# Seven block products for Q in the first half too, with every instruction of the schedule put at a new place

## The chip, the cores and the metric

The kernel runs on one core of a Trainium2 chip. The time is device microseconds from the first to the last instruction of an execution, with the little that lies around them; it is the median of several executions. The profile is of one execution.

## The reference

The input x has 2048 rows of 640. Everything works on its layer norm xn.

- Attention: Q = xn·wq, for 32 heads of 128. Only the last 512 keys and values of the cache are used. Per head, softmax(Q·Kᵀ/√128)·V, then the heads' results times wo, summed over the heads.
- Gate: relu(xn·w1 + b1)², times w2, plus b2, through silu, with 1728 hidden columns.
- Output: x + attention · gate.

All of it is in float32. TensorE multiplies a rounded kind of float32 (fp32r), so each operand is split into a high part and a low remainder, and each product is made of three matmuls: high·high, high·low, low·high (`triple`, L601).

## The kernel before

**Tiles and stages.** The rows of x are four tiles of 512. First comes the gate: tile 0 with plain products, tiles 1 and 2 together with seven block products in place of eight (a Winograd form of Strassen's scheme, on 2×2 blocks), then their second products in 28 steps of `c_down`, during which the layer norm of tile 3 is made. Then comes attention in 128 **units** (L997 and after); a unit is one head times one tile. The first 64 units (first half) take tiles 0 and 3, the last 64 (second half) tiles 1 and 2. Four units in a row, two heads times two tiles, make a group; there are 16 groups to a half.

**A unit.** TensorE makes 12 matmuls of scores (`s_mm`, four chunks of keys, three matmuls each), 12 of softmax times V (`v_mm`), Q for a later unit (`q_mm`, 15 matmuls; in the second half `q_prod` and `q_rest`), and a share of the output product (`r_mm`, 30 matmuls for each pair of heads and tile). VectorE folds the maximum over the keys out of each chunk's scores (`max_fold`), subtracts it (`shift`), adds up; ScalarE takes the exponentials and splits off high parts; GpSimd makes the low parts.

**Q in the second half.** Two heads are one block dimension, two tiles the other, and the contraction over 640 is two blocks of 256 and a rest of 128. With the weights' sums s1 to s4 and the tiles' sums t1 to t4, a group's Q takes 7 products of 6 matmuls and 4 rests of 3: 54 matmuls in place of 60. The weights' sums are made by GpSimd in the first half, when the same heads' weights are there anyway (`q_sums`), and stored to DRAM; in the second half they are loaded in four pieces (`q_piece`).

**What sets the order.** All work of attention is entered in a list with a time in a nominal unit of PERIOD = 12.4 (`at`, `on`), and a table K of some hundred small numbers moves single entries. The list is sorted by that time (L2007) and the calls are made in that order; every engine then takes its instructions strictly in it. The nominal times have no other effect.

**The slots of TensorE's code.** TensorE's instruction stream is fetched in blocks of 256 slots. Each matmul of the program becomes two instructions, a weight load and a matmul, one slot each; a wait for more than one semaphore adds slots of its own, one for each two further semaphores. `addr_align(256, slot)` asks that the next instruction stand at that slot of a block; the stream is filled up to it with empty instructions, up to 255 of them. In attention each unit asks for five places:

```
SLOTS = (0, 11, 22, 33, 42)
for c in range(KC):
    on(0.68 * c, align, i, SLOTS[c])
    on(0.68 * c, s_mm, i, c)
on(0.68 * KC - 0.6, align, i, SLOTS[KC])
# align: pe.addr_align(256, (188 + 128 * i + slot) % 256)
```

So a unit has 128 slots. The four chunks of scores begin 11 slots apart, and each is 6 slots of instructions and 5 of fill, when nothing else stands between. After the fifth place 86 slots are left for the other 42 matmuls of a unit of 54 (84 slots). If the stream is already past the place that is asked for, it is filled up to that place in the next block. The steps of `c_down` ask for places of their own (`lead_slot`), and the last of them, slot 139 before step 20, is followed by 150 matmuls up to unit 0.

Of the kernel before, what the change touches and what calls it, by code (L numbers as in the profile page):

```python
# [8 lines left out]
F32 = mybir.dt.float32  # L9
# [5 lines left out]
P = 128  # L15
NT = 512
# [2038 lines left out]
```

## Time and profile before

| | |
|---|---|
| median of 3 runs | 1973.06 us (1970.76 to 1973.12) |
| profiled execution, its own time | 1971.29 us |
| its span | 1969.5 us, 30081 instructions |
| TensorE (PE) busy | 1939.7 us, 98%, 8489 matmuls |
| VectorE (DVE) busy | 1708.3 us, 87% |
| GpSimd (POOL) busy | 1479.0 us, 75% |
| ScalarE (ACT) busy | 1394.5 us, 71% |
| mean granted TensorE clock | 0.995 |

All instructions are recorded under one line, that of a helper that fixes the order (L127), so the rows are told apart by the names of their tiles: s are scores, q Q, pq the bank in which Q is made, pt the split exponentials, o softmax times V, ot the split result of two heads, r their output product, acc the sum, e the shifted scores and exponentials, rdm and rds the folds. PE rows are matmuls, PEld rows weight loads. A matmul's duration in a row is longer than the distance to the next one, since they overlap. The gate takes the first 290 us, attention the time up to about 1880 us.

### The profile page before, as it was taken

How to read it: one execution, taken by the hardware profiler on the slowest of the kernel's cores; microseconds unless marked ns; L12 is line 12 of the kernel's file. 1: busy time of each engine (PE TensorE's matmuls, PEld its weight loads, DVE VectorE, ACT ScalarE, POOL GpSimd, SP SyncE). 2: the span in 40 equal slices, each digit the busy share in tenths (PEclk: the TensorE clock that was granted, in tenths of full speed). 3: DMA queues.
4: the chain of work that ended last, by engine and by line, in shares of the span. 5: the costliest groups of instructions: out<-in, count | busy, mean ns of one | idle time of the engine just before them, and what ended most of it. 6: DMA issues, size and time to landing. Idle time of an engine off the chain costs nothing. (4 is left out here: it accounts for less than half of the span.)

```text
span 1969.5 us, 30081 instructions
## 1 busy us (share of the span) xinstructions
PE 1939.7 (98%) x8489; PEld 1588.9 (81%) x8489; DVE 1708.3 (87%) x2915; ACT 1394.5 (71%) x2994; POOL 1479.0 (75%) x895
## 2 busy tenths in 40 slices
PE   9999999799999999999999999999999999999998
PEld 7888887588888888888888888888888888888787
DVE  6864747599999999999999989999999999999865
ACT  5675538577777777777777787777777777777743
POOL 1022118599999999999998688999998888888952
PEclk9999999899999999999999999999999999999999
DMA  6865953132222222333323333333332222222355
GB/s 204 278 227 206 369 184 120 64 97 97 97 97 97 97 97 97 99 107 108 106 97 110 116 126 99 105 105 105 105 114 84 84 84 84 83 84 89 123 180 192
DMA packets 149025, 246.89 MB, mean 125 GB/s; under 512 B 13876, under 2 KB 70726, under 8 KB 147846
## 3 DMA queue, kind: packets, MB, share of 16 engines
q1 hardware_dynamic: 144998, 229.87, 35.5%
q0 software_dynamic: 3728, 14.94, 2.0%
q8 instruction: 78, 1.28, 0.3%
q14 instruction: 77, 0.63, 0.1%
q10 hardware_dynamic: 144, 0.16, 0.0%
HBM read 175.97 MB, written 68.96 MB: 124 GB/s over the span
## 5 line engine op out<-in xcount | busy, mean ns | idle before, releaser
L127 POOL TENSOR_TENSOR pt<-e,pt 128x1024 fp32r<-128x1024 f32 x256 | 616.8, 2410 | 146.7 <-ACT pt L127 143.8
L127 PE MATMUL r<-ot,wo 128*128 128x512 f32 x1920 | 496.5, 392 | 3.0 <-DVE q L127 3.0
L127 PEld LDWEIGHTS r<-ot,wo 128*128 128x128 f32 x1920 | 361.5, 188 | 83.3 <-DVE q L127 3.5
L127 PE MATMUL o<-pt,wv 128*128 128x512 f32 x1536 | 395.3, 395 | 2.2 <-POOL pt L127 2.2
L127 PE MATMUL s<-q,wk 128*128 128x512 f32 x1536 | 371.9, 391 | 15.5 <-issue 15.5
L127 DVE TRANSPOSE_TENSOR_REDUCE rdm<-s 128x16 f32<-128x512 f32 x512 | 349.0, 713 | 35.1 <-PE s L127 33.5
L127 PEld LDWEIGHTS s<-q,wk 128*128 128x128 f32 x1536 | 289.5, 189 | 77.7 <-issue 16.2
L127 PEld LDWEIGHTS o<-pt,wv 128*128 128x128 f32 x1536 | 287.0, 188 | 72.2 <-POOL pt L127 7.0
L127 DVE TENSOR_TENSOR e<-s,bm 128x512 f32<-128x512 f32 x512 | 317.5, 655 | 2.5 <-POOL pt L127 0.7
L127 POOL TENSOR_TENSOR e<-e,e 128x1024 f32<-128x1024 f32 x128 | 307.9, 2405 | 8.9
L127 ACT ACTIVATE e<-e 128x1024 f32<-128x1024 f32 x256 | 269.7, 1054 | 32.8 <-DVE e L127 32.0
L127 ACT ACTIVATE pt<-e 128x1024 fp32r<-128x1024 f32 x256 | 271.5, 1060 | 16.1 <-PE o L127 0.9
L127 DVE TENSOR_TENSOR acc<-r,acc 128x512 f32<-128x512 f32 x300 | 203.4, 678 | 35.8 <-PE r L127 30.6
L127 PE MATMUL pq<-ax,wq 128*128 128x512 f32 x960 | 231.4, 389 | 0.0
L127 PEld LDWEIGHTS pq<-ax,wq 128*128 128x128 f32 x960 | 180.1, 188 | 37.9 <-DVE q L127 0.3
L127 ACT ACTIVATE rdm<-rdm 32x64 f32<-32x64 f32 x384 | 97.8, 255 | 97.3 <-DVE rdm L127 92.6
L127 ACT ACTIVATE rowm<-rowm 32x16 f32<-32x16 f32 x384 | 82.1, 214 | 89.6 <-DVE rowm L127 86.5
L127 DVE TRANSPOSE_TENSOR_REDUCE rds<-e 128x32 f32<-128x1024 f32 (+1 forms) x128 | 123.8, 968 | 17.2 <-POOL e L127 16.8
L127 ACT ACTIVATE rds<-rds 32x32 f32<-32x32 f32 (+1 forms) x384 | 89.4, 233 | 54.4 <-DVE rds L127 49.9
L127 ACT ACTIVATE rows<-rows 32x16 f32<-32x16 f32 x384 | 82.2, 214 | 60.5 <-DVE rows L127 52.0
L127 DVE TENSOR_TENSOR o<-o,bs 128x512 f32<-128x512 f32 x128 | 88.7, 693 | 11.0 <-PE o L127 3.9
L127 POOL TENSOR_TENSOR wo<-or,wo 128x640 fp32r<-128x640 f32 x62 | 97.4, 1571 | 0.0
(463 smaller groups left out, 2877.7 us busy)
## 6 DMA issues: line engine op xcount, KB each, us to landing
or<-in_wo_dram SPq DMA_DIRECT2D x62, 320.0 KB
qp<-wq_d SPq DMA_DIRECT2D x30, 640.0 KB
kr<-in_kT_dram SPq DMA_DIRECT2D x62, 256.0 KB
vr<-in_v_dram SPq DMA_DIRECT2D x62, 256.0 KB
wq_d<-ss SPq DMA_DIRECT2D x60, 256.0 KB
qp<-wq_d SPq DMA_DIRECT2D x30, 512.0 KB
wq_d<-wq SPq DMA_DIRECT2D x30, 384.0 KB
qr<-in_wq_dram SPq DMA_DIRECT2D x32, 320.0 KB
```

The costliest lines, as they stand in the source:

```text
L127: ins = method(*args, **kwargs)
```

## The change

- **Q in the first half.** From group 2 on (unit 8), the first half's Q also comes from seven products; only groups 0 and 1 keep `q_mm` (`NQS = UPG * G`). That takes 14 times 6 = 84 matmuls out: 8405 in place of 8489.
- **Tile sums for tiles 0 and 3.** `outer_sum`, `outer_hi`, `outer_lo` make t1 to t4 for these tiles during steps 10 to 18 of `c_down`: 12 sums and 8 low parts of 128×512 on VectorE, 8 high parts on ScalarE; 8 loads of tile 0 and 16 stores of 256 KB on GpSimd's queue. Six tiles of sums stay in SBUF in each half (`open_t`).
- **Weight sums.** `stage_raw` to `part_keep` take the place of `q_sums` to `q_store`. For all 16 groups the weights are loaded, summed, split and stored, and both halves load the pieces: 1051 DMA issues on SP's queue in place of 752.
- **Score banks in pairs.** A tile of scores now spans two banks. `max_fold` and `shift` work on 128×1024: 2 instructions each per unit in place of 4.
- **SBUF.** pt, the tile sums and other moving operands come to stand at multiples of 512 bytes; in the built program the 1536 matmuls that read pt had it 128 bytes beyond one, and 288 that read tile sums 256 bytes beyond one. The split results stay in four fixed tiles.
- **Places.** K has 1380 entries in place of 280, most of them for single units (`@56`), and a third set, part 2, for units 6 to 63.

The diff, cut to its core:

```diff
-    -0.06, "Q41": 1.2, "Q51": 0.05, "Q61": -0.15, "Q71": 0.17, "Q81": -0.21, "Q91": -0.62,
...
+    "Q8@59": 0.5, "Q8@63": -1.37, "Q8@67": 2.27, "Q8@7": -1.15, "Q91": 0.28, "Q92": 0.33,
+    "Q920": -1.66, "Q9@124": -0.99, "Q9@56": 0.14, "Q9@60": 0.05, "Q9@64": 0.08, "R00": -0.38,
...
+    def outer_sum(q, k):
+        if k == 0:
+            outer_tiles(q)
+        t0, t1, t2, t3 = (raw(t[1]) for t in TO[q])
+        x, b12, b22 = XO[q], XC[LATE, q], XC[LATE, NQ2 + q]
+        out, one, two, op = (
+            (t0, b12, x[:, 0, 0, :], ALU.subtract),
...
+        ENG["o"].tensor_tensor(out, one, two, op=op)
...
+    def outer_lo(q, j):
+        hi, lo = TO[q][j]
+        ENG["l"].tensor_tensor(lo, raw(lo), raw(hi), op=ALU.subtract)
+        for i in range(2):
+            pool.dma_start(TS_d[0][j][:, q, i, :], raw(TO[q][j][i]))
...
-    NQS = NU // 2 - UPG
+    NQS = UPG * G
...
+    def stage_lo(g, k):
+        hi, s = ST[g, k]
+        pool.tensor_tensor(s.bitcast(F32R), s, raw(hi), op=ALU.subtract)
...
+    def stage_keep(g, k):
+        n, lo = SUM_AT[k]
+        for i, src in enumerate((raw(ST[g, k][0]), ST[g, k][1])):
+            sp.dma_start(wq_d[g][n][:, i, lo : lo + NQ2, :], src)
...
     def s_mm(i, c):
         hf, g, t, h = units[i]
-        SC[i, c] = pools["psb"].tile([P, NT], F32, tag="s", name=f"s{i}_{c}", bufs=KC)
+        if c % 2 == 0:
+            SC[i, c // 2] = pools["psb"].tile(
+                [P, 2, NT], F32, tag="s", name=f"s{i}_{c}", bufs=KC // 2
+            )
...
-    def shift(i, c):
...
+    def shift(i, k):
...
+        dve.tensor_tensor(
+            E[i, k], SC.pop((i, k)), MB[i][:, None, :].to_broadcast([P, 2, NT]), op=ALU.subtract
+        )
...
+        part = 0 if i < NQS - 2 else 2 if i < NU // 2 else 1
+
         def key(name, when, u=0):
             return sum(
-                (K.get(f"{name}{k}", 0.0) for k in (hf, f"{hf}{(i + u) % UPG}", f"@{i + u}")), when
+                (K.get(f"{name}{k}", 0.0) for k in (part, f"{part}{(i + u) % UPG}", f"@{i + u}")), when
             )
...
-        if NG <= n < HALF * NG:
+        if NQS // UPG <= n < HALF * NG:
...
                 on(key("Q9", 2.75), q_prod, n, 2, "a", 3, "t3")
...
-        for c in range(KC):
-            on(0.8 + 0.68 * c, max_fold, i, c)
+        for k in range(KC // 2):
+            on(key(f"mf{k}", 1.5 + 1.3 * k), max_fold, i, k)
```

The order of TensorE's instructions, at three places. An ISA row is an `addr_align`; it takes no slot itself, and what it fills isn't shown. A MATMUL row is two slots for each matmul.

The first place is unit 8, the first whose scores stand beside the new Q products. Before, its second to fourth chunks of scores, each with its place ahead of it:

```order
L127 ISA
L127 MATMUL s8_1_4124<-q8_0_3931,wk0_4_0_3873 128x512
L127 MATMUL s8_1_4124<-q8_1_3932,wk0_4_0_3873 128x512
L127 MATMUL s8_1_4124<-q8_0_3931,wk0_4_1_3874 128x512
L127 ISA
L127 MATMUL s8_2_4136<-q8_0_3931,wk0_4_0_3873 128x512
L127 MATMUL s8_2_4136<-q8_1_3932,wk0_4_0_3873 128x512
L127 MATMUL s8_2_4136<-q8_0_3931,wk0_4_1_3874 128x512
L127 ISA
```

Now the same chunks (`s8_2` is the pair of banks of chunks 2 and 3; `ta` holds the tile sums, `pq2a` is Q's bank):

```order
L312 ISA
L312 MATMUL s8_0_4156<-q8_0_4096,wk0_4_0_3940 128x512
L312 MATMUL s8_0_4156<-q8_1_4097,wk0_4_0_3940 128x512
L312 MATMUL s8_0_4156<-q8_0_4096,wk0_4_1_3941 128x512
L312 ISA
L312 MATMUL s8_2_4171<-q8_0_4096,wk0_4_0_3940 128x512
L312 MATMUL s8_2_4171<-q8_1_4097,wk0_4_0_3940 128x512
L312 MATMUL s8_2_4171<-q8_0_4096,wk0_4_1_3941 128x512
L312 MATMUL pq2a_3909<-ta_3068,qp2_2_4026 128x512 x6
L312 ISA
L312 MATMUL s8_2_4171<-q8_0_4096,wk0_4_0_3940 128x512
```

The six matmuls of the product with t3 (Q9 at 2.75 + 0.33 − 1.66 = 1.42) have come ahead of the fourth chunk's place (2.04). They make 12 slots, and two waits 2 more, where 5 slots were free: 20 slots stand where 11 are asked for, so the stream is filled up with 256 − 9 = 247 empty instructions. The same stands in every fourth unit from 8 to 60, 14 times.

The second place is unit 4, before, where three matmuls of scores and six of the output product stand between two places:

```order
L127 ISA
L127 MATMUL s4_0_3543<-q4_0_3365,wk0_2_0_3307 128x512
L127 MATMUL s4_0_3543<-q4_1_3366,wk0_2_0_3307 128x512
L127 MATMUL s4_0_3543<-q4_0_3365,wk0_2_1_3308 128x512
L127 MATMUL r1_0_3547<-ot0_3301,wo0_0_0_3110 128x512 x2
L127 MATMUL r1_0_3547<-ot0_3301,wo0_0_1_3111 128x512
L127 MATMUL r1_0_3547<-ot1_3440,wo0_1_0_3256 128x512 x2
L127 MATMUL r1_0_3547<-ot1_3440,wo0_1_1_3257 128x512
L127 ISA
L127 MATMUL s4_1_3559<-q4_0_3365,wk0_2_0_3307 128x512
```

These are 18 slots where 11 are asked for, and 249 are filled; it is the only such place before. Now the rows read:

```order
L312 ISA
L312 MATMUL s4_0_3594<-q4_0_3414,wk0_2_0_3371 128x512
L312 MATMUL s4_0_3594<-q4_1_3415,wk0_2_0_3371 128x512
L312 MATMUL s4_0_3594<-q4_0_3414,wk0_2_1_3372 128x512
L312 ISA
L312 MATMUL s4_0_3594<-q4_0_3414,wk0_2_0_3371 128x512
L312 MATMUL s4_0_3594<-q4_1_3415,wk0_2_0_3371 128x512
L312 MATMUL s4_0_3594<-q4_0_3414,wk0_2_1_3372 128x512
L312 ISA
```

Here nothing stands between, and the fill is 5 again.

The third place is the way into attention, with the semaphores that an instruction waits for. Before, the first Q product and the first scores; 150 matmuls and 5 waits stand between slot 139 and slot 188, and no fill is needed (139 + 305 = 444 = 256 + 188):

```order
L127 MATMUL py2_4_2537<-ch26_1_2828,cw26_0_2831 128x512
L127 MATMUL py2_4_2537<-ch26_0_2827,cw26_1_2832 128x512
L127 MATMUL pq0_2899<-ax0_0_0_2735,wq0_2797 128x512 [waits DMASW4_49,DMASW5_49,DMASW3_49,DMASW6_49,DMASW2_49,DMASW7_49,DMASW1_49,DMAHW1_49,DMASW0_49,PE_49]
L127 MATMUL pq0_2899<-ax0_0_1_2736,wq0_2797 128x512 [waits DMAHW1_49]
L127 MATMUL pq0_2899<-ax0_0_0_2735,wq0_2797 128x512 x2
```

Now:

```order
L312 MATMUL py2_4_2593<-ch26_1_2891,cw26_0_2894 128x512
L312 MATMUL py2_4_2593<-ch26_0_2890,cw26_1_2895 128x512
L312 MATMUL pq0_2977<-ax0_0_0_2840,wq0_2898 128x512 [waits DMASW5_49,DMASW4_49,DMASW6_49,DMASW3_49,DMASW7_49,DMASW2_49,DMAHW0_49,DMASW1_49,DMAHW3_49,DMASW0_49,DMAHW5_49,PE_49,Activation_49]
L312 MATMUL pq0_2977<-ax0_0_1_2841,wq0_2898 128x512 [waits DMAHW6_49]
L312 MATMUL pq0_2977<-ax0_0_0_2840,wq0_2898 128x512 [waits DVE_49]
```

The first Q matmul waits for 13 semaphores in place of 10, one slot more, so the stream is one slot past slot 188 when unit 0 asks for it, and 255 are filled.

Two more such places come with the change: unit 5, where three matmuls of softmax times V stand between the first two chunks (fill of 254), and unit 124, where the product with t3 stands ahead of the fifth place (fill of 246). All other fills are of 20 slots or fewer, as before. Together, the fills are 3035 slots before and 7186 now.

More of the change, by code (lines that the diff above doesn't have):

```diff
@@ L157 @@
     TILE = ((0, LATE), (T1, T2))
-    TS_d = [dpool.tile([P, DC // 2, 2, NT], F32, name=f"ts_d{k}") for k in range(4)]
+    TS_d = [
+        [dpool.tile([P, DC // 2, 2, NT], F32, name=f"ts_d{hf}_{k}") for k in range(4)]
+        for hf in range(2)
+    ]
     wq_d = [
@@ new lines, in stage_sum, with stage_hi @@
+        if k in (1, 2):
+            out = pools["ep"].tile([P, NQ2, DH], F32, tag="zs", name=f"zs{g}_{k}", bufs=1)
+        else:
+            out = a21
+        ST[g, k] = [SPARE[k in (0, 3)], out]
+        one, two, op = (
+            lambda: (a21, a22, ALU.add),
+            lambda: (ST[g, 0][1], a11, ALU.subtract),
+            lambda: (a11, a21, ALU.subtract),
+            lambda: (a12, ST[g, 1][1], ALU.subtract),
+        )[k]()
+        pool.tensor_tensor(out, one, two, op=op)
+    def stage_hi(g, k):
+        hi, s = ST[g, k]
+        act.activation(hi, s, AF.Copy)
@@ L1102, in q_right @@
         if what in ("t2", "t3", "t4"):
-            what = f"{what}{q}"
-            return QR[f"{what}x" if n == NG and f"{what}x" in QR else what]
+            return QR[f"{what}{q}"]
         t, c = RES[what]
-        return [x[:, c + q, :] for x in XT[1, t]]
+        return [x[:, c + q, :] for x in XT[0, t]]
     def q_prod(n, k, b, blk, what, start=False):
@@ L1257, in s_add @@
         pool.tensor_tensor(E[i, 0], E[i, 0], E[i, 1], op=ALU.add)
-        if units[i][0] and not K.get("one"):
+        if units[i][0]:
             a, b = (E[i, 0][:, k, :] for k in range(2))
@@ L1293, in o_hi @@
     def o_hi(i):
-        two = keep.tile([P, 2, D], F32R, tag="ot", name=f"ot{i}", bufs=2 * G)
+        two = OTS[i % (2 * G)]
         OT[i] = [two[:, k, :NT] for k in range(2)]
@@ L1491, in late_down @@
         if f == 0 and 0 in ds:
-            for k in range(4):
-                LPY[k] = pools["psb"].tile([P, NT], F32, tag="s", name=f"ly{k}", bufs=KC)
+            for k in range(0, 4, 2):
+                two = pools["psb"].tile([P, 2, NT], F32, tag="s", name=f"ly{k}", bufs=KC // 2)
+                LPY[k], LPY[k + 1] = two[:, 0, :], two[:, 1, :]
             LPY[4] = psx.tile([P, NT], F32, tag="x", name="ly4")
@@ L1613 @@
                 c_prep(m + 2, k)
+        for f, *a in OUTER.pop(m, ()):
+            f(*a)
         c, odd = divmod(m - 2, 2)
@@ L1621 @@
                 spill(LATE, XS[LATE], slice(c - 1, c))
-        if m == OPEN:
+        if m == 0:
+            octx = ExitStack()
+            pools["to"] = octx.enter_context(tc.tile_pool(name="outer", bufs=1, side="right"))
+        if m == first_m - 2:
+            outer_load(0)
+        if m == first_m + int(len(steps) / per / 2) - 1:
+            outer_load(1)
+        if m == OPEN + int(K.get("OO", 0)):
+            for f, *a in [w for n, l in sorted(OUTER.items()) if n >= m for w in l]:
+                f(*a)
+            OUTER.clear()
+            octx.close()
             pools["ep"] = ctx.enter_context(tc.tile_pool(name="early", bufs=1, side="right"))
@@ L1685 @@
             ):
-                if (n or kind in "vo") and not (hf and kind == "q"):
+                if (n or kind in "vo") and (n < 2 or kind != "q"):
                     at(base + when - 10.5, load_raw, kind, hf, h)
                     at(base + when + K.get(f"P{kind}{hf}{j}", 0.0), prep, kind, hf, h)
-    at(10.0, pad, pools["ep"], 480)
     tra = ExitStack()
-    for k in ("tra", "tz"):
-        pools[k] = tra.enter_context(tc.tile_pool(name=k, bufs=1))
+    pools["tra"] = tra.enter_context(tc.tile_pool(name="tra", bufs=1))
+    OTS.extend(
+        keep.tile([P, 2, D], F32R, tag="ot", name=f"ots{n}", bufs=2 * G) for n in range(2 * G)
+    )
+    open_t()
     def turn_end():
@@ L1728 @@
[L1728 to L1752 removed]
+    ORDER = [*range(2, NG), 0, 1]
@@ new lines @@
+    BM, BS = 0.85, 8.3
+    for hf, b, places in (
+        (
+            0,
+            0,
+            (
+                (1, BM, ("t20",)),
+                (1, BS, ("t21",)),
+                (2, BM, ("t30",)),
+                (2, BS, ("t31",)),
+                (4, BM, ("t40", (0, 2))),
+                (4, BS, ("t41", (0, 3))),
+                (6, BM, ((1, 0),)),
+                (6, BS, ((1, 1),)),
+            ),
+        ),
+        (
+            1,
+            NU // 2,
+            (
+                (-5, BM, ((0, 2),)),
+                (-5, BS, ((0, 3),)),
+                (-4, BM, ((0, 0),)),
+                (-4, BS, ((0, 1),)),
+                (-3, BM, ((1, 0), "t20")),
+                (-3, BS, ((1, 1), "t21")),
+                (-2, BM, ((0, 4), "t30")),
+                (-2, BS, ("t31",)),
+                (-1, BM, ("t40", (1, 2))),
+                (-1, BS, ("t41", (1, 3))),
+                (0, BM, ((1, 4),)),
+            ),
+        ),
+    ):
+        for u, when, pieces in places:
+            for what in pieces:
+                if isinstance(what, str):
+                    at((b + u) * PERIOD + when + 0.05, load_t, hf, what)
+                else:
+                    for i in range(2):
+                        at((b + u) * PERIOD + when + 0.05, load_x2, hf, what[0], i, what[1])
@@ L1804 @@
             qs = [(i + 2, {1: 5.6, 3: 4.9}.get(i, 4.2), 6.4 if i == 1 else 4.1)]
-        for n, q_at, low in qs if i + AHEAD < NU // 2 else ():
+        for n, q_at, low in qs if i + AHEAD < NQS else ():
             for c in range(DC):
```

315 lines of the change are left out of this document (139 added, 176 removed), and 274 rows, old and new, of tables (K, QP_OF).

## The prediction

> **What bounds the kernel now.** I read the page's busy shares and slices first, then stretches of the span, then the one stretch where TensorE isn't full.
>
> ```profile
> PE 1939.7 (98%) x8489; PEld 1588.9 (81%) x8489; DVE 1708.3 (87%) x2915; ACT 1394.5 (71%) x2994; POOL 1479.0 (75%) x895
> PE   9999999799999999999999999999999999999998
> PEclk9999999899999999999999999999999999999999
> ```
>
> ```profile
> 220.00:230.00 10.00, 10.00 (x45) 8.29 (x45) 5.77 (x9) 4.49 (x8) 1.62 (x3) 1.00 1.04 418
> 240.00:250.00 10.00, 10.00 (x46) 8.27 (x45) 4.79 (x8) 4.72 (x8) 0.00 (x0) 1.00 0.80 284
> 300.00:400.00 100.00, 81.48 (x339) 65.74 (x339) 64.78 (x107) 65.75 (x140) 73.56 (x46) 0.90 0.28 90
> 400.00:1050.00 650.00, 650.00 (x2846) 533.72 (x2845) 621.24 (x1027) 493.32 (x1111) 599.15 (x370) 1.00 0.30 98
> 1500.00:1850.00 350.00, 350.00 (x1530) 286.27 (x1529) 331.07 (x583) 267.87 (x591) 307.41 (x162) 1.00 0.28 92
> ```
>
> In each row of the second fence come the length, then the busy time of PE, PEld, DVE, ACT and POOL, the granted clock, the DMA share and GB/s. TensorE never idles from 400 to 1050 us nor from 1500 to 1850, at full clock. So TensorE is the bound, at 650/2846 = 0.228 us a matmul; DVE (621/650 = 96%) and POOL (92%) are close behind. Only 300 to 400 differs: 339 matmuls stand there, and at 0.228 there would be about 439. About 23 us are lost. The timeline of TensorE shows where:
>
> ```profile
> start us, us, engine line op out<-in xcount [idle before <-releaser]
> 336.68 0.87 PE L127 MATMUL s<-q,wk 128*128 128x512 f32 x3
> 340.58 2.93 PE L127 MATMUL r<-ot,wo 128*128 128x512 f32 x6 [3.04 <-DVE q L127]
> 358.99 4.18 PE L127 MATMUL s<-q,wk 128*128 128x512 f32 x9 [15.48 <-issue]
> 362.96 1.43 PE L127 MATMUL r<-ot,wo 128*128 128x512 f32 x3
> ```
>
> Three matmuls of scores, then, after a wait for Q, six of the output product, and then 15.48 us of nothing that ends by "issue": no semaphore ended it. This is unit 4, and just here, between the six matmuls and the next scores, the stream of before has its only long fill, 249 empty instructions. Counting slots over the built program gives 3035 filled ones in all; with 2 × 8489 for matmuls and about a hundred waits that is 20,200 slots or 78.9 blocks of 256. The profile's instruction queue agrees:
>
> ```profile
> q8 instruction: 78, 1.28, 0.3%
> ```
>
> 78 fetches of 16.4 KB. So I read the pause as TensorE's sequencer working through 249 empty instructions with nothing behind them to run.
>
> **The price of a long fill.** The six matmuls are issued when their wait ends, at 340.58, and the next scores start at 358.99: 18.4 us for 249 fills, 74 ns each. Then nine matmuls take 362.96 − 358.99 = 3.97 us where nine at 0.228 take 2.05: after the pause the array runs slow for a while, 1.9 us lost. Against that stands the work already handed to TensorE when the fill begins, its cover; here the six matmuls, worth 1.4 us at full rate. So a long fill of n slots loses
>
> 18.4 × n/249 + 1.9 − cover.
>
> With the cover of 1.4 that is 18.9 us for this one. In the usual unit a fill of 20 slots (1.5 us) leaves no idle time from 400 to 1050, so the cover is at least 1.5 there. It can't be more than part of a unit (54 matmuls, 12.3 us), because each unit's scores wait for Q and for banks that the other engines set free in the same unit; half of that, 6.1, is my upper bound. At the changed place nine matmuls (2.1 us) stand between the last place and the fill, and something is queued ahead of them: I take 4, about two such batches, nearer to the row that was seen than to the bound.
>
> **The change part by part.**
>
> *84 matmuls out*: 84 × 0.228 = −19.2 us, all on the bound.
>
> *The long fill of unit 4 goes* (its order now leaves the usual fill of 5): −18.9 us.
>
> *New long fills.* The product with t3 has come between the third and fourth chunks of scores in 14 units (8, 12 to 60): 247 slots each, 18.25 + 1.9 − 4 = 16.15 us, in all 226.1. Three single ones: unit 0 (255 slots: 16.7), unit 5 (254: 16.7), unit 124 (246: 16.1), in all 49.5. Sum +275.6 us. With a cover of 6.1 it is 240; with 1.4 it is 320. Other engines hide nothing of it. They idle along, because the fourth chunk of scores comes late, and behind it on TensorE wait the second half of Q's product, the output product and softmax times V. But those wait for work that was finished during the pause, so I add nothing for what is late next; the row of 300 to 400 bears this out, since its loss of 23 us is the 18.9 and the 3.04 before it to about a microsecond.
>
> *pt and the tile sums at multiples of 512 bytes.* Groups by form, mean ns last but two:
>
> ```profile
> L127 PE MATMUL r<-ot,wo 128*128 128x512 f32 x1920 | 496.5, 392 | 3.0 <-DVE q L127 3.0
> L127 PE MATMUL o<-pt,wv 128*128 128x512 f32 x1536 | 395.3, 395 | 2.2 <-POOL pt L127 2.2
> L127 PE MATMUL s<-q,wk 128*128 128x512 f32 x1536 | 371.9, 391 | 15.5 <-issue 15.5
> L127 PE MATMUL pq<-ax,wq 128*128 128x512 f32 x960 | 231.4, 389 | 0.0
> ```
>
> The matmuls that read pt take 395 ns, those whose operands were already in place 389 to 392. If they come down to 389: 1536 × 6 ns = −9.2 us. Bounds: 0, if it isn't the place; −18, if r and s (3 × 1920 + 2 × 1536 ns more) come down as well. I take −9.2, because only pt moves.
>
> *Folds and shifts in pairs.*
>
> ```profile
> L127 DVE TRANSPOSE_TENSOR_REDUCE rdm<-s 128x16 f32<-128x512 f32 x512 | 349.0, 713 | 35.1 <-PE s L127 33.5
> L127 DVE TENSOR_TENSOR e<-s,bm 128x512 f32<-128x512 f32 x512 | 317.5, 655 | 2.5 <-POOL pt L127 0.7
> L127 DVE TRANSPOSE_TENSOR_REDUCE rds<-e 128x32 f32<-128x1024 f32 x64 | 78.4, 1225 | 0.9 <-POOL e L127 0.9
> ```
>
> A fold of 1024 columns took 1225 ns where two of 512 take 1426, so a unit saves about 0.4 us of folds, and as much of shifts by the same ratio. Against it stand the additions for Q in the first half, which the second half already has (331/350 = 95%). DVE stays under TensorE: 0 on the path. Two banks are now held until one 1.2 us shift ends, at worst half of it, 0.6 us, a unit; but s waits for nothing but "issue" now, so I take 0. Were that cover gone, the scores would be late, and with them the next fold.
>
> *Tile sums during the second products.*
>
> ```profile
> L127 DVE TENSOR_TENSOR xT<-xc,xT 128x512 fp32r<-128x512 f32 x15 | 10.3, 689 | 3.5 <-ACT xT L127 3.5
> L127 ACT ACTIVATE xT<-xc 128x512 fp32r<-128x512 f32 x15 | 9.4, 629 | 25.8 <-DVE xc L127 25.8
> ```
>
> 20 DVE instructions at 689 ns are 14 us over 30 us of steps in which DVE is busy about half; 8 ACT ones at 629 add 5. The DMA is the tighter cover: 24 transfers of 256 KB are 6.3 MB, at 418 GB/s 15 us, added where the queues are full (1.04) until 240 us. After that 20% and more is free, and the weights come three steps ahead (three times 15 matmuls, 10 us). Cost 0 to 15; I take 2. Late next would be the weights and hidden tiles of `c_down`, and TensorE with them.
>
> *Weight sums anew.* POOL's additions and low parts are the same columns as before, and the first half now has pauses in which it can catch up. The 299 more DMA issues are on SP's queue, in attention, where the DMA engines are 0.30 busy. 0.
>
> **Sum.** The profiled execution's own time is 1971.3 (span 1969.5). 1971.3 − 19.2 − 18.9 + 275.6 − 9.2 + 2 = 2201.6, and the median of the runs shown stands 1.8 us above that execution: **2203 us**, 12% slower.
>
> **Rivals.**
>
> *A. A long fill costs no more than a short one.* Then the pause at 343 us has another cause. For it: "issue" names nothing, and 20 filled slots a unit pass unseen from 400 to 1050. Against it: the pause stands at the very place of the only long fill, and the count of blocks fits. The time: 1971.3 − 19.2 − 9.2 + 2 = 1945, with the pause still there, or 1926 without it; faster by 1.4 to 2.4%. [...] The row of 15.48 us speaks against it. Chance 6%.
>
> *B. Every pause has an aftermath.* The softmax of the unit whose fourth chunk came late holds up its low parts on POOL (92% busy) and so softmax times V a unit later. For it: PE waited for pt now and then (2.2 us in all).
>
> ```profile
> L127 POOL TENSOR_TENSOR pt<-e,pt 128x1024 fp32r<-128x1024 f32 x256 | 616.8, 2410 | 146.7 <-ACT pt L127 143.8
> L127 ACT ACTIVATE e<-e 128x1024 f32<-128x1024 f32 x256 | 269.7, 1054 | 32.8 <-DVE e L127 32.0
> ```
>
> Price: fold 1.2, shift 1.2, exponential and high part 1.05 each and low part 2.4 are 6.9 us, with the small steps on the maxima some 9, and the plan leaves 17 of its units; if TensorE caught up fully, some 3 us would be lost each time, 17 × 3 = 51: 2254 us. Against it: after 363 us nothing of the kind shows. Chance 7%.
>
> *C. The one-slot and two-slot overruns don't occur* (units 0 and 5), because a wait is counted otherwise in the built code: 2203 − 33 = 2170. The count of blocks fits to within a block, which bounds such an error but doesn't exclude it. Chance 5%.
>
> **How the numbers follow.** Forecast 82%, A 6%, B 7%, C 5%. The cover (6.1 to 1.4) moves the forecast from 2167 to 2247, the operand places by 9 either way, the DMA by up to 13 up. The middle of these, 2165 to 2245, holds most of the forecast and all of C; A and most of B lie outside. The median can tell 0.2% from no change. Only A ends on the other side: faster 6%, within 0.2% 1%, slower 93%.
>
> **What would show it.** PE's slices below 9 all through the first half, and full from half-way on but for one near the end. 17 idle times of 13 to 17 us before PE rows ended by "issue", 16 of them before s (14 every four units, some 64 us apart: 210 matmuls and a pause), one before r. Each followed by matmuls at half rate, and PEclk lower there. 94 instruction fetches in place of 78, since 4151 more slots are filled. 8405 matmuls; those that read pt near 389 ns. The forecast is wrong if the fills stand in the code and PE doesn't pause, or if it pauses with another releaser.

## The result: 2243 us, 13.7% slower

The changed kernel takes 2243.09 us (median of 4, 2241.83 to 2243.3), the kernel before 1972.05 beside it (1970.76 to 1973.12): a ratio of 1.1373, 95% interval 1.1354 to 1.1393. That is 40 us above the predicted 2203 and 2 us under the top of its range. The profiled execution took 2243.27 us, its span 2241.3.

The page of the profile after: busy time of the engines, TensorE's 40 slices, the clock granted to it, and the queue that fetches instructions (packets, MB, share).

```profile
PE 1952.5 (87%) x8405; PEld 1594.3 (71%) x8405; DVE 1676.9 (75%) x2451; ACT 1425.2 (64%) x3096; POOL 1493.9 (67%) x971
...
PE   9999977787777788777778879999999999999798
...
PEclk9999989898888898888889889999999999999899
...
q8 instruction: 94, 1.54, 0.3%
```

84 matmuls are gone, and yet TensorE's share fell from 98 to 87%. It isn't full any more in the whole first half of attention, where the clock dips too (0.88 of full speed from 400 to 1050 us), and it is again in the second half, but for the slice with unit 124's pause and the last one, which was an 8 before as well. 94 blocks of code are fetched in place of 78; 4151 slots more of fills, less 168 of matmuls, are 15.6 blocks of 256. The view of waits of TensorE (total us, times, longest) and the rows of two stretches that were full before:

```profile
PE s L312 <- issue: 252.6, 17, 17.1
PE r L312 <- issue: 16.2, 1, 16.2
PE o L312 <- POOL pt L312: 3.5, 9, 0.5
PE py L312 <- DVE ch L312: 3.3, 1, 3.3
PE py L312 <- ACT cw L312: 2.0, 1, 2.0
```

```profile
250.00:300.00 50.00, 44.43 (x177) 35.04 (x177) 24.09 (x36) 18.61 (x30) 7.00 (x13) 0.93 0.82 309
400.00:1050.00 650.00, 492.30 (x2067) 401.72 (x2066) 448.63 (x622) 387.43 (x892) 442.85 (x302) 0.88 0.35 108
```

268.8 us are idle by "issue", nearly all of the difference of 271 us. One of the 17 entries for s is of 0.19 us, so there are 16 pauses before s and one before r. From 400 to 1050 us 2067 matmuls are done where 2846 were. And 250 to 300 us, still in the second products of the gate, isn't full either; it was before:

```profile
250.00:300.00 50.00, 50.00 (x221) 41.20 (x220) 25.06 (x37) 21.96 (x40) 7.53 (x11) 1.00 0.56 193
```

The timeline of TensorE in unit 8, one of the 14 units with the product with t3 (start, us, work):

```profile
434.55 2.20 PE L312 MATMUL s<-q,wk 128*128 128x512 f32 x9
436.59 1.52 PE L312 MATMUL pq2a<-ta,qp 128*128 128x512 f32 x6
453.55 1.62 PE L312 MATMUL s<-q,wk 128*128 128x512 f32 x3 [15.43 <-issue]
454.96 1.48 PE L312 MATMUL pq2a<-ax,qp 128*128 128x512 f32 x3
456.24 1.03 PE L312 MATMUL r<-ots,wo 128*128 128x512 f32 x3
```

Three chunks of scores, the six matmuls with t3, then 15.43 us that no semaphore ended, then the fourth chunk; and its three matmuls take 454.96 − 453.55 = 1.41 us where 0.68 is the rate, at a granted clock of 0.62 (453.55 to 457.55 us). The pauses of units 0 and 5:

```profile
315.54 5.10 PE L312 MATMUL s<-q,wk 128*128 128x512 f32 x12 [14.60 <-issue]
397.69 4.18 PE L312 MATMUL s<-q,wk 128*128 128x512 f32 x9 [17.12 <-issue]
```

### The profile page after: what moved, and what is told of

Its sections match the earlier page's. It is cut to its first block, busy times and chain, and to the rows that moved or that the text cites. A ratio compares the mean times of both kernels' runs of the same rounds, so it can differ in the third digit from the quotient of the medians.

```text
span 2241.3 us, 34382 instructions
## 1 busy us (share of the span) xinstructions
PE 1952.5 (87%) x8405; PEld 1594.3 (71%) x8405; DVE 1676.9 (75%) x2451; ACT 1425.2 (64%) x3096; POOL 1493.9 (67%) x971
## 5 line engine op out<-in xcount | busy, mean ns | idle before, releaser
L312 PE MATMUL s<-q,wk 128*128 128x512 f32 x1536 | 386.9, 400 | 253.0 <-issue 252.6
L312 DVE TRANSPOSE_TENSOR_REDUCE rdm<-s 128x32 f32<-128x1024 f32 x256 | 315.4, 1242 | 310.0 <-PE s L312 301.8
L312 PE MATMUL r<-ots,wo 128*128 128x512 f32 x1920 | 503.1, 399 | 16.4 <-issue 16.2
L312 PEld LDWEIGHTS r<-ots,wo 128*128 128x128 f32 x1920 | 371.5, 194 | 98.5 <-issue 16.6
L312 PE MATMUL o<-pt,wv 128*128 128x512 f32 x1536 | 384.1, 391 | 4.4 <-POOL pt L312 3.5
L312 DVE TENSOR_TENSOR e<-s,bm 128x1024 f32<-128x1024 f32 x256 | 301.7, 1183 | 2.6 <-POOL pt L312 1.5
L312 POOL TENSOR_TENSOR wv<-vr,wv 128x512 fp32r<-128x512 f32 x62 | 80.6, 1300 | 227.9 <-ACT wv L312 227.9
L312 POOL TENSOR_TENSOR gr<-gr,ots 128x256 fp32r<-128x256 f32 (+1 forms) x112 | 73.5, 664 | 52.5 <-ACT ots L312 52.3
L312 PE MATMUL py<-ch,cw 128*128 128x512 f32 x410 | 98.2, 400 | 6.1 <-DVE ch L312 3.3
L312 PEld LDWEIGHTS py<-ch,cw 128*128 128x128 f32 x410 | 78.9, 194 | 25.0 <-DVE ch L312 3.7
```

Source lines behind the costliest of these rows:

```text
L312: ins = method(*args, **kwargs)
```

## The experiments

Times are medians. The kernel before ran beside each group of runs, at 1971.33 (the first four), 1970.86 (the next four), 1971.27 (the next three) and 1971.59 us (the last). In "loss" below I count, over the starts of all matmuls, how much the distance to the next one exceeds 0.2267 us.

### The product with t3 put back behind the fourth chunk

```diff
-    "Q920": -1.66,
+    "Q920": -0.9,
```

> The changed kernel with one number altered: in units 8 to 60 the product with t3 stands behind the fourth chunk of scores and its place, so the 14 fills of 247 slots become ordinary ones; the three single long fills stay. The theory (a long fill stops TensorE for the time that its sequencer takes over the empty instructions, 16 us, and leaves it slow for some 2 us more): 2243 - 14 x 18 = 1991 us, 80 code fetches, three idle times by 'issue'. The rival (the pause belongs to the product with t3, which comes too early for its operands): the product still stands in the same stretch of the unit, the pauses move behind it, and the time stays near 2243.

2011.26 us, 1.0204 of before (1.0189 to 1.0219). The 14 pauses of the groups are gone, and those of units 0, 5 and 124 are left. In this run and the next, VectorE's sum of Q's bank (u3) stands ahead of the product with t3, which is then missing from that sum; the instructions are the same in number. It is 20 us above what I expected. Those 20 us show again in the next run.

### No fill over 14 slots in the changed kernel

```diff
-FIRST_SLOT = 188
+FIRST_SLOT = 190
-    "Q9@124": -0.99,
+    "Q9@124": -0.85,
-    "v@4": -0.04,
+    "v@4": -0.3,
```

> The changed kernel without any long fill: as the run before, and the product with t3 of unit 124 behind the fifth place, softmax times V of unit 3 ahead of unit 5, and all places of attention two slots later, so that the one slot too many ahead of unit 0 no longer matters. The largest fill is 14 slots. The theory: 2243 - 17 x 18 = 1937 us, faster than the kernel before by 35 us, with no idle time by 'issue'. From the parts of the prediction without fills: 1971 - 19 (matmuls) - 19 (fill of unit 4) - 9 (operand places) + 2 = 1926; what lies above that is lost outside the fills. The rival (Q by blocks in the first half, or the wider tiles, hold TensorE up by themselves and the pauses hid that): 1960 or more.

1958.57 us, 0.9934 (0.9919 to 0.9948). TensorE waits for "issue" no more. The three fills were worth 2011.26 − 1958.57 = 52.7 us, 17.6 each, close to the 16.5 predicted for them. The kernel is now faster than before, but 22 us above the 1937 that I expected and 33 above the 1926 that the prediction's sum gives without fills. The view of waits shows where some of it lies: in each of 13 groups TensorE waits for VectorE's sum (qu), which stands in the order just before the product with t3. Two of the 13 rows:

```profile
PE pq6a L312 <- DVE qu L312: 1.2, 1, 1.2
PE pq12a L312 <- DVE qu L312: 1.2, 1, 1.2
```

### The kernel before without its long fill

```diff
-    "R0@1": 1.19,
+    "R0@1": 1.0,
```

> The kernel before with one number altered: the first output product of units 0 and 1 stands ahead of unit 4 and not between its first two chunks of scores, so that its fill of 249 slots is gone. The theory: 1972 - 19 = 1953 us, and the idle time of 15.48 us by 'issue' is gone; with it may go part of the 3.04 us wait ahead of it. The rival (the pause comes from the late Q of unit 4 and not from the fill): the pause stays and the time is within 2 us of 1972.

1954.76 us, 0.9916 (0.99 to 0.9933): 16.6 us less for one number in the table. The timeline at the place of the pause:

```profile
340.68 2.93 PE L127 MATMUL r<-ot,wo 128*128 128x512 f32 x6 [3.74 <-DVE q L127]
343.41 4.28 PE L127 MATMUL s<-q,wk 128*128 128x512 f32 x12
347.52 1.54 PE L127 MATMUL r<-ot,wo 128*128 128x512 f32 x6
```

The scores follow the output product at once, with no 15 us between. But these 12 matmuls still take 347.52 − 343.41 = 4.11 us where 2.72 is the rate: the slow stretch that I had put down to the fill comes behind the 3.74 us wait for Q alone as well. With the wait itself, which is 0.7 us longer than before (3.04), that is most of the difference between the 18.9 us that I took for this fill and 16.6.

### Fills half as long

```diff
-        pe.addr_align(BLOCK, (FIRST_SLOT + BLOCK // 2 * i + slot) % BLOCK)
+        pe.addr_align(BLOCK // 2, (FIRST_SLOT + BLOCK // 2 * i + slot) % (BLOCK // 2))
```

> The changed kernel, with the places of attention asked for in blocks of 128 slots in place of 256; the order is the same, but an overrun is filled up to the same place half a block later. The 17 long fills become 14 of 119, and 127, 126 and 118 slots. The theory (74 ns a slot, less a cover of 2.2 us, and 1.9 us of slow matmuls after each): 119 x 0.074 - 2.2 + 1.9 = 8.5 us each, 17 x 8.5 = 145 us above the run without long fills, about 2080 us. The rival (an overrun costs a fixed time, that of fetching code anew, whatever is filled): 2243 again.

2083.36 us, 1.057 (1.0554 to 1.0586). The 17 long fills are each shorter by 128 slots, everything else stands as in the changed kernel, and the pauses have shrunk with them:

```profile
PE s L312 <- issue: 101.6, 17, 7.8
PE r L312 <- issue: 6.9, 1, 6.9
```

17 × 128 = 2176 slots made 2243.09 − 2083.36 = 159.7 us: 73 ns a slot, as the 74 ns of the one fill of before. So the price goes with the number of empty instructions. That an overrun costs a fixed time, whatever is filled, is excluded by this run.

### No long fill, and t3 ahead of the sum

```diff
-    "Q1020": -0.9,
+    "Q1020": -0.5,
```

on top of the run without long fills.

> The version without a fill of over 14 slots, with VectorE's sum of Q's bank put 0.40 later in the order, behind the product with t3 (2.41 against 2.18), as the changed kernel has it; nothing is left out of the computation now. Theory (the fills carry the loss, and the 20 us by which the run without long fills stayed above its sum were TensorE waiting in each group for that sum, thirteen times 1.3 us): 1958.6 - 13 x 1.3 = 1942 us, no wait of TensorE for qu, and what is left over the sum (some 10 us) lies at 230 to 290 us. Rival (TensorE's queue is short of about 1.5 us in each group whatever stands there, so that the wait only moves to the next product): 1958 us, with as many pauses of about 1.5 us beside the products.

1947.05 us, 0.9878 (0.9861 to 0.9894). The waits for the sum are gone but for one of 0.8 us, and the time falls by 11.5 us, 5 less than I expected; 21 us above the 1926 are left. Set against the changed kernel this run says what is won by taking all 17 long fills out: 2243.09 − 1947.05 = 296.0 us, 17.4 each. Set against the kernel before it shows the rest of the change without them. The losses of TensorE by stretch, us:

| | before | this run |
|---|---|---|
| 200 to 300 (c_down) | 0.2 | 10.8 |
| 300 to 450 | 23.9 | 5.4 |
| 450 to 1850, by distances under 0.245 us | 11.4 | 2.1 |
| 450 to 1850, by longer ones (waits) | 3.5 | 15.0 |

With 84 × 0.2267 = 19.0 us for the matmuls taken out, these rows give −24.7 of the −24.9 us by which the spans differ. Two rows are gains that I had counted (the fill of unit 4, the places in SBUF), and two are losses that I had not, but for 2 us: 10.6 us in c_down, and 11.5 us of waits.

### c_down: the sums on GpSimd

```diff
+    "OE": 1, "OL": 1,
```

(the outer tile sums and their low parts on GpSimd), on the run before.

> The run with t3 before the sum, with the stage of the outer tile sums (their sums and the subtractions for their second halves) on GpSimd in place of VectorE; transfers, their bytes and their order are unchanged. Tells apart two causes of the 10 us that TensorE loses at 230 to 290 us. If VectorE (full from 225 to 250 us: 21.2 of 25 us) prepares weights and activations late, its 8 us of sums go and TensorE's waits of 230 to 290 us fall from about 10 to under 3 us: some 8 us less than the run with t3 before the sum. If the transfers are late (the DMA engines 0.93 to 0.98 busy from 200 to 250 us), nothing changes: within 2 us of that run, since the sums are slower on GpSimd but their stores are as many.

1955.74 us, 0.9924 (0.9909 to 0.9939): 8.7 us slower than on VectorE, where I had expected 8 less or no change. The loss of 200 to 300 us is 18.6. The waits of 225 to 300 us:

```profile
ACT to L312 <- POOL to L312: 13.6, 4, 7.0
...
PE py L312 <- DVE cw L312: 4.0, 3, 1.7
PE py L312 <- ACT cw L312: 3.7, 2, 3.4
PE py L312 <- DVE sg L312: 3.6, 1, 3.6
```

GpSimd's sums take 1.3 to 1.9 us where VectorE's take 0.7, and ScalarE, which also splits the weights, stands behind them for 13.6 us. VectorE became slower too: most of its subtractions beside GpSimd's sums take 1.6 to 1.9 us, and the same instructions between them 0.7 to 0.8.

```profile
232.00 1.78 DVE L312 TENSOR_TENSOR ch<-ch,ch 128x512 fp32r<-128x512 f32 x1
245.08 0.67 DVE L312 TENSOR_TENSOR ch<-ch,ch 128x512 fp32r<-128x512 f32 x1
```

So this run put new delays in place of the old and tells the two causes apart less well than I had meant.

### c_down: the sums sooner

```diff
-    "OM": 10,
+    "OM": 7, "OP": 2.0,
```

> The run with t3 before the sum, with the stage of the outer tile sums begun three steps sooner and with two pieces of work in each step in place of three (steps 7 to 19 in place of 10 to 18), so that its loads and stores stand over more time, and sooner, where the DMA engines are at 0.57 to 0.69. If the transfers are what comes late, the waits of 230 to 290 us fall by half or more: 5 to 8 us less than the run with t3 before the sum. If VectorE is late because of its sums, the same gain is to be had here, so this run decides only together with the one on GpSimd; if neither gains, the loss is from the opening of the attention's tiles at about 250 us, which both leave where it is.

1949.24 us, 0.9888 (0.9873 to 0.9902), within 2.2 us of the run with t3 before the sum; the loss of 200 to 300 us stays, at 11.3. Spreading a little changes nothing, whichever cause it is.

### P's tiles at 128 bytes past a multiple of 512 again

```diff
     ap = ctx.enter_context(tc.tile_pool(name="at", bufs=2))
+    pad(ap, 64)
```

> The run with t3 before the sum, with 64 bytes more ahead of the attention's tiles, so that the tiles of P (pt) and the tile sums begin 128 bytes past a multiple of 512 again, as pt did before the change; instructions and fills are the same. Prediction's term: 1536 matmuls of pt at 6 ns, 9 us slower than the run with t3 before the sum, with the mean of pt's matmuls at 395 in place of 389 ns. My reading of the changed kernel's trace: 13 us slower, since the excess over 226.7 ns for each matmul fell in the whole of the attention, not under pt alone. Rival (places do nothing, the mean of pt's matmuls falls for other reasons): within 2 us.

1950.27 us, 0.9895 (0.988 to 0.9909): 3.2 us slower, not 9 or 13. The waits of TensorE's weight loads from 450 to 1000 us, with the places of the change and then in this run:

```profile
PEld s L312 <- DVE q L312: 4.3, 11, 0.4
PEld o L312 <- POOL pt L312: 3.8, 11, 0.7
```

```profile
PEld o L312 <- POOL pt L312: 0.8, 3, 0.4
PEld s L312 <- DVE q L312: 0.7, 4, 0.2
```

The matmuls do become slower: the distances under 0.245 us lose 14.8 us from 450 to 1850, against 2.1. But with the good places TensorE waits once in each group (11 groups in this stretch) for the low part of Q and once for P, and most of what the places give goes there. With P at 128 bytes past, the distances over 0.245 us lose 4.9 us from 450 to 1850 in place of 15.0. The kernel before has no such wait from 450 to 1000 us.

### c_down: two buffers, and the attention's tiles opened a step sooner

```diff
-    "OM": 10, "OO": 1,
+    "OM": 7, "OP": 2.5, "OO": 0,
-    ..., name=f"xo{q}", bufs=1)
+    ..., name=f"xo{q}", bufs=2)
-        if m == first_m + int(len(steps) / per / 2) - 1:
+        if m == first_m - 1:
             outer_load(1)
```

> The run with t3 before the sum, with the outer tile sums from step 7 on at 2.5 pieces a step, both quarters of x loaded ahead of them into two buffers (one before), and the opening of the attention's first tiles one step sooner, where it was before the change. Theory by now (the loss at 230 to 290 us is neither VectorE's work nor the spread of the bytes, which the two runs on that left as it was: VectorE stands behind the load of the second quarter, 4.7 us in the run with the early stage, and SyncE's queue behind the tiles that this stage gives back late, so that the last weights of c_down are issued after the attention's first loads): the waits of 230 to 290 us fall from about 10 to under 4 us, 1941 us. Rival (the DMA engines are full whatever the order): the same waits, 1947 us.

1947.85 us, 0.9883 (0.9867 to 0.9899): no gain. But the waits have moved, and they tell the mechanism. VectorE's timeline in the run with t3 before the sum, and then in this one:

```profile
249.00 0.82 DVE L312 TENSOR_TENSOR cw<-cw,cw 128x640 fp32r<-128x640 f32 x1
254.81 0.69 DVE L312 TENSOR_TENSOR to<-xo,to 128x512 f32<-128x512 f32 x1 [4.98 <-DMA ts_d<-to]
255.53 0.69 DVE L312 TENSOR_TENSOR to<-to,xo 128x512 f32<-128x512 f32 x1
256.14 0.68 DVE L312 TENSOR_TENSOR ch<-ch,ch 128x512 fp32r<-128x512 f32 x1
```

```profile
240.63 0.68 DVE L312 TENSOR_TENSOR to<-to,xo 128x512 f32<-128x512 f32 x1
241.35 0.69 DVE L312 TENSOR_TENSOR to<-xc,to 128x512 f32<-128x512 f32 x1
242.59 3.38 DVE L312 SCALAR_TENSOR_TENSOR sg<-py,b_sb,sg 128x512 f32<-128x512 f32 x5 [0.55 <-ACT sg L312]
```

In the first, a sum (to) overwrites a tile whose store (ts_d) hasn't landed; VectorE stands 4.98 us, and ch, two places behind that sum in its order, starts at 256.14; TensorE's wait for ch there is 3.2 us. The changed kernel shows the same with a stop of 4.73 us: there ScalarE's part of ch was done at 250.5 us, and TensorE stops for ch at 253.8 us. In this run the sums come without a stop, and the five gate products that set TensorE's banks free stand behind them: TensorE waits 4.5 us for sg. The wait for cw at 282 us, 2.2 us before, is under 1 us, with the opening of the attention's tiles one step sooner.

### No fills in the attention at all

```diff
     def align(i, slot):
-        pe.addr_align(BLOCK, (FIRST_SLOT + BLOCK // 2 * i + slot) % BLOCK)
+        return
```

on the run with t3 before the sum.

> The run with t3 before the sum, with no fill in the attention at all (c_down keeps its own): about 2800 empty slots fewer, and each block of 256 slots ends wherever the program has come to. If the fills of a few slots are hidden, as I took them, and their places keep the crossing of a block away from TensorE's waits, this is slower than with them: a crossing every 256 slots, some 60 of them in the attention, each open at a wait for up to 2 us as the aftermath of the long ones, at most 60 x 2 = 120 us, and 10 to 40 us by my estimate. If neither the fills nor the places do anything in the changed kernel, within 2 us.

1947.03 us, 0.9874 (0.986 to 0.9888): the same to 0.02 us. The page:

```profile
PE 1921.6 (99%) x8405; PEld 1568.1 (81%) x8405; DVE 1670.2 (86%) x2451; ACT 1425.0 (73%) x3096; POOL 1494.8 (77%) x971
...
q8 instruction: 67, 1.10, 0.2%
```

Ten blocks fewer are fetched than in the run with the fills (77), each block ends where it happens to end, and TensorE's busy time is the same to 0.1 us. The short fills are hidden, as I took them; but they buy nothing here, and my 10 to 40 us for leaving them out was wrong.

### The places in SBUF alone, in the kernel before

```diff
     ap = ctx.enter_context(tc.tile_pool(name="at", bufs=2))
+    pad(ap, 192)
```

> The kernel before, with 192 bytes more ahead of the attention's tiles: P's tiles (pt) begin at multiples of 512 bytes, as in the changed kernel; the old tile sums, which stood 256 past one, stand 128 past one. Nothing else is changed, the long fill of unit 4 stays. Prediction's term: 1536 matmuls of pt at 6 ns, 9.2 us less, 1961.9 us. By the traces of the changed kernel (the excess of each stretch of 50 us falls from 0.40 to 0.10 us, over 31 of them): 9 us less as well, if nothing else stops TensorE. By the run with pt at 128 past (3.2 us, since other waits came in the excess's place): 3 us less. Rival (places do nothing): within 1 us.

1963.67 us, 0.9956 (0.9942 to 0.997): 7.6 us less, from moving tiles by some bytes. The groups of TensorE from 450 to 1000 us, before and in this run (us, mean ns):

```profile
L127 PE MATMUL r<-ot,wo 128*128 128x512 f32 x669 | 174.7, 391 | 0.0
...
L127 PE MATMUL o<-pt,wv 128*128 128x512 f32 x535 | 137.0, 394 | 0.0
```

```profile
L127 PE MATMUL r<-ot,wo 128*128 128x512 f32 x672 | 174.4, 389 | 0.0
...
L127 PE MATMUL o<-pt,wv 128*128 128x512 f32 x540 | 135.2, 389 | 0.0
```

The predicted step by itself is there, 394 to 389 ns in this stretch, and r, whose operands stand at multiples of 512 bytes in both, comes down by 2 ns with it. Little comes in its place here: from 450 to 1850 us the distances over 0.245 us lose 5.1 us, 3.5 before.

### c_down: one piece of work in each step

```diff
-    "OM": 7, "OP": 2.5,
+    "OM": 7, "OP": 1.0,
```

on the run with two buffers; the loads of x stand three steps and more ahead.

> The run with the two buffers, with the outer tile sums at one piece of work in each step of c_down, from step 7 to 32, in place of 2.5 (and with both quarters of x loaded at least three steps ahead). Theory (VectorE works in order: in the run with t3 before the sum it stands 4.98 us at a sum that overwrites a tile whose store, ts_d<-to, hasn't landed, and TensorE then waits 3.6 us for ch; in the run with two buffers it is full from 225 to 242 us with sums, and the five gate products, sg, stand behind them, for which TensorE waits 4.5 us): with one piece a step neither is in the way of ch, cw and sg, so TensorE's waits of 225 to 290 us fall to under 3 us and the time to 1940 us. Rival (the DMA engines, 0.91 to 0.98 busy from 200 to 275 us, set the loss, whatever VectorE does): the same 9 to 10 us are lost, 1947 us.

1956.14 us, 0.9919 (0.9905 to 0.9932): 8.3 us slower than the run with two buffers, where I had expected 8 less. The waits of TensorE and of SyncE's queue from 225 us on, and the stretches (columns as before; the last but one is the DMA share):

```profile
PE py L312 <- ACT cw L312: 14.3, 2, 13.8
```

```profile
SPq L312 <- DMA ts_d<-to: 19.9, 4, 17.9
```

```profile
225.00:250.00 25.00, 25.00 (x112) 20.71 (x111) 21.23 (x32) 16.00 (x27) 8.64 (x16) 1.00 0.95 307
250.00:275.00 25.00, 25.00 (x112) 20.70 (x111) 16.17 (x24) 10.10 (x16) 6.97 (x13) 1.00 0.67 252
```

Two things are seen apart now. From 225 to 275 us TensorE doesn't stop, for the first time since the change; 3.1 us are lost from 200 to 225 instead, where the run with two buffers loses 0.6. Up to 250 us the DMA engines are as busy as in that run (0.95 and 0.93), so its wait for sg at 239 us was VectorE's order, as the theory said, and not the bytes. For ch the timeline of VectorE above says the same; whether full DMA engines made the store late that VectorE stood for, no run tells. And the edit does not give one piece a step to the end: at step 21, where the attention's tiles open, the kernel makes what is left of the sums at once, here the whole second quarter, VectorE's 10 instructions of it from 264 to 271 us. So the sums end later, their tiles are given back later, and the attention's first tiles take their place: the load of those stands in SyncE's queue for 17.9 us until the last store of the sums (ts_d) has landed, with the last weights cw behind it, and TensorE waits 13.8 us for these at 276 us. Both orders would have to be right at once; a kernel that loads those weights ahead of the attention's tiles was not run.

## Why the prediction was right, and where its sizes were off

The sum was 2203, the time 2243. The trace of the changed kernel says where the 40 us lie. Counted as loss over the starts of the matmuls, a pause being a distance of over 5 us and the 25 matmuls behind it counted with it, the terms are, in us:

| | in the sum | by the traces, before and after |
|---|---|---|
| the 17 long fills | +275.6 | +307.0 (271.3 idle, 35.7 slow behind) |
| the fill of unit 4 | −18.9 | −18.4 |
| 84 matmuls | −19.2 | −19.0 |
| attention beside the pauses | −9.2 | −8.5 (22.4 to 13.9) |
| tile sums (c_down) | +2 | +11.0 |
| together | +230.3 | +272.1; the spans differ by 271.8 |

So the fills missed by 31 us, c_down by 9. Both lie inside the bounds given for them, but both on the slow side, and the time is only just inside the range.

**What bounds it, and the cause of the pause.** Right. Without the one long fill the kernel before has no pause; with half the slots the idle time by "issue" falls from 268.8 to 108.5 us.

**74 ns a slot.** Right: 73 by the run with half fills.

**The cover of 4 us.** Mis-sized; it is the term that failed in the price of a fill. It came out of two batches of matmuls, one of them "something queued ahead". In unit 8 the six matmuls with t3 start at 436.59 and the next scores at 453.55: 16.96 us, of which 1.36 is their own work. So about 15.6 us are idle of the 18.2 that the fill takes at 74 ns a slot; over all 17 fills, 4213 slots, 271.3 of 312 are. That is a cover of 2.4 us each: the nine matmuls (2.0 us) that stand between the fourth chunk's place and the one before, and little else. With the 2.1 us of slow matmuls behind each pause a fill costs 18.1 in the changed kernel. The 17.4 by difference is less: with the pauses gone, the first half of attention loses 12.9 us, where it loses 4.1 beside them. The two overruns in units 0 and 5 stand in the timeline, with pauses of 14.60 and 17.12 us.

**84 matmuls.** Right: 8405, at 0.2267 us.

**The fill of unit 4 that goes.** Right: in the changed kernel that pause and the slow matmuls behind it, 18.4 us, are gone. Alone, in the kernel before, it was worth 16.6, since the slow matmuls belong to the wait for Q as well, and stay there.

**pt and the tile sums, −9.2.** The step was right where TensorE is the bound: −7.6 us alone, and the losses under 0.245 us fell by 9.3 in the run with t3 before the sum. But in the changed order without pauses it is worth 3.2, since TensorE then waits for other engines. In the changed kernel the row of the table agrees with it partly by luck: distances under 0.245 us lose 11.9 us less than before, longer ones 3.4 more. There the matmuls of P come down as forecast (450 to 1000 us):

```profile
L312 PE MATMUL o<-pt,wv 128*128 128x512 f32 x408 | 99.5, 389 | 0.2 <-DVE ots L312 0.2
```

**Folds and shifts in pairs, weight sums: 0.** Nearly right in the changed kernel, whose long pauses may give the other engines time to catch up: beside the pauses its waits in attention are only the 3.4 us longer. Without the long fills a term shows that the sum lacked: 11.5 us of waits that weren't there before, in the first half for the low part of Q (VectorE) and for P (GpSimd), about 0.7 us a group for both. Most of it stands there only because the places made TensorE faster (4.9 in place of 15.0 us with P at 128 bytes past). Which of the edits makes Q and P late (the pairs, the seven products' additions, the new places in the order) wasn't tried and stays open.

**Tile sums during the second products, +2.** Mis-sized, and by a wrong mechanism: 11.0 us in the changed kernel, 10.6 without its pauses. The bound of 15 held. I had costed VectorE by its share of busy time and called the transfers the tighter cover. What the runs show at work is the order on two queues, though full DMA engines may be behind the late store: the wait of VectorE for a store, with ch behind it, and the wait of SyncE's queue for tiles to be given back, with cw behind it. The wait that the change adds there, on a tile with a single buffer, I hadn't looked for.

**The rivals.** A, a long fill as cheap as a short one, is excluded by the run with half fills, at 73 ns a slot; 18.4 us stood between the last issue and the next matmul in the kernel before. What spoke for it, that the short fills pass unseen, holds: the run without fills, which crosses its blocks at any place, takes 1947.03 us, and the one with them 1947.05. B, 3 us more for each pause, is refuted by the trace: beside the pauses and the 25 matmuls behind each, the first half of attention loses 4.1 us in all, 11.0 before. C, the overruns in units 0 and 5 that don't occur, is refuted by the two pauses, 14.60 and 17.12 us; in unit 0 the one slot for three more semaphores was enough.

**What would show it.** All of it stands in the profile after: 16 pauses before s and one before r, 14.6 to 17.1 us long; some 66 us apart in the groups (64 forecast); slow matmuls behind each; 94 fetches; o at 389 ns from 450 to 1000 us.

**The faster versions.** The run with t3 before the sum, 1947.05 us, beats both kernels by 1.2% and 13%, and without any fill it is as fast. But the two small edits to the kernel before, no long fill (−16.6) and the places (−7.6), would add up to about 1947 as well; they were not run together. By that sum the seven products in the first half are worth nothing here as they are ordered: the 19 us of matmuls that they save are lost again in c_down and in waits. That stays a sum; it wasn't measured.

## What to carry to other kernels

Where code is filled up to a place in a block, count the instructions that can come to stand between two places: here one slot too many ahead of unit 0 made a fill of 255, and TensorE stood for 14.60 us; over the 17 long fills it was idle for 271.3 of the 312 us that they take at 74 ns a slot. And try the kernel without any fill first: here the run without fills took 1947.03 us, and the one with the short fills 1947.05. A new stage that is costed by its engines' shares of busy time can still be late by order alone, as the tile sums were here (2 us in the sum, 11.0 in the trace): for each instruction that it adds, ask what it waits for, a store out of its own single buffer and a tile not yet given back among them, and what stands behind it on that queue.

## What the runs showed of the hardware that was not expected

- In the long fills an empty instruction cost 73 to 74 ns (159.7 us for 2176 of them, 18.4 us for 249), yet the short fills of attention, ten blocks of code by the fetches (77 with them, 67 without), cost the kernel nothing (1947.05 us with, 1947.03 without), and nor did the places at which blocks of code are crossed there.
- Slow matmuls stand behind waits for semaphores too, not only behind a pause by "issue". In the kernel before without its long fill twelve took 4.11 us in place of 2.72 behind a wait of 3.74 us. In the kernel before the granted clock was 0.50 from 340.58 to 343.50 us, behind the wait of 3.04 us and ahead of the pause. In the changed kernel, behind a wait of 1.95 us with shorter ones after it, it was 0.50 from 287 to 289 us, and 0.83 over 280 to 290.
- The matmuls of 128x512 that read pt took 394 ns with pt 128 bytes past a multiple of 512 and 389 with it at one (450 to 1000 us, the kernel before and the run with the places alone), and r, whose operands stood at multiples of 512 both times, went from 391 to 389 ns with them.
- Beside GpSimd's sums most of VectorE's subtractions of the same kind took 1.6 to 1.9 us, and 0.7 to 0.8 between them.
